# Reordering the first nine slots of a fused sparse-attention and feed-forward kernel

## Chip, cores and metric

The kernel runs on one core of a Trainium2 chip. The metric is the device time of one execution in microseconds (us). Its engines appear in the profile as PE (TensorE matmul), PEld (its weight loads), DVE (VectorE), ACT (ScalarE), POOL (GpSimd) and SP (SyncE, which here only issues DMAs). Each engine works through its own instructions strictly in the order in which the program gives them.

## What is computed

For 8 batches of 576 tokens with 8 heads of width 64, the reference computes causal attention. Heads 0 to 3 see the last 32 positions, heads 4 to 7 see the earlier positions of the same residue modulo 32. The result, 4608 tokens by 512, goes through a multiplicative feed-forward block:

```
scores = where(mask[h], q @ k.T / sqrt(64), -1e9)      # mask local for h < 4, strided for h >= 4
attn   = softmax(scores) @ v                            # (8, 8, 576, 64)
x      = attn.transpose(0, 2, 1, 3).reshape(4608, 512)
out    = ((x @ w1) * (x @ w2)) @ w3 @ w_out             # w1, w2: 512x1024; w3: 1024x1024; w_out: 1024x512
```

## The kernel before

**Slots.** The attention is cut into 32 pairs of heads (four pairs for each batch: two local, two strided). The main loop `for n in range(NP + 2)` has one slot for each pair, and a pair passes through the slots as a hand-written pipeline. For a pair, `load_qk` fetches q and k with a cast to fp16 (DMAs issued by POOL), `load_v` fetches v (issued by SP), and then:

- `emit_T` transposes q and k on PE (`tpq`, `tpk`) and copies them out as `qT`/`kT`. A local pair uses two ACT copies (L274). A strided pair uses one DVE copy `qTS` (L278) and one ACT copy (L279).
- `emit_S` makes the scores on PE (`sp`) and adds the mask on DVE in two halves (L305, `tmp`).
- `emit_max` and `emit_sub` are DVE passes (L313, L320), `emit_exp` is one ACT pass (L332).
- `emit_norm` takes row sums and reciprocals on DVE (L340, L342) and scales on POOL (L343).
- `emit_cast_v` casts v to fp16 on POOL (L254, `vh`).
- `emit_P` transposes the probabilities on PE (`pp`) and copies them on ACT (`pT`, L356 local, L363 strided).
- `emit_V` multiplies by v on PE (`op`) and copies into `xT`, on ACT for a local pair (L378), on ACT and DVE for a strided one (L392, L394, L396).

In a steady slot n of the kernel before, PE runs S(n), V(n-2), T(n+1), then P(n-1), with feed-forward pieces between them.

**Feed-forward pieces.** `w3 @ w_out` is folded once into one matrix `wfh`: for each of 8 row blocks `fold_t` transposes w3 on PE (`w3tp`, L207) and copies it on ACT (L209, `w3T`), and `fold_m` runs eight matmuls (`fps`, L216) and one ACT copy (L218, `wfh`). The tokens form 9 chunks of 512. For each chunk `emit_a` and `emit_b` run eight times each, four matmuls apiece (`aps` L225, `bps` L235). ACT copies a (L229, `asb`), DVE multiplies (L238, `abt`). `emit_out` runs four times per chunk, eight matmuls apiece (`ops`, L243), then an ACT copy (L246) and a store on SP.

**Credit.** `feed(us, batches)` hands out pieces in program order against a credit: `T_A` = 0.87 for an a or a b, twice that for an out or a `fold_m`, 0.6 for a `fold_t`. `next_piece` prefers a and b pieces whose tokens are complete (`full` counts finished batches), gives folds when there is none, and allows outs only when no fold is left. All of this happens when the program is built, so it sets each engine's order and nothing else.

**Shared buffers.** `psA` has two PSUM buffers, used by `tpq`, `tpk`, `pp` and `w3tp`; `psF` has six, used by all other matmuls. `s16`, the landing tile of q and k, has four. A DMA that POOL issues takes one of eight completion semaphores in turn, so that issue i waits on POOL until issue i-8 has landed.

## Time and profile before

| | |
|---|---|
| time, median of 3 runs | 309.9 us (309.56 to 310.26) |
| the profiled execution: its own time / its span | 311.65 us / 309.4 us |
| mean granted TensorE clock in it | 0.989 |
| busy: PE, DVE, ACT, POOL | 273.5, 187.1, 174.1, 145.3 us |
| chain that ended last: PE, DMA, DVE | 65%, 14%, 10% of the span |
| DMA: software queue (POOL), hardware queue (SP) | 14.88 MB, 21.24 MB |

The span is the time from the first to the last instruction of the profiled execution; the time of that execution has 2.25 us more around it. Busy time of PE counts overlapping matmuls once. Slots are told apart in the trace by their mask additions (`tmp`, L305) or their score matmuls (`sp`, L299).

### The profile page before, as it was taken

The page shows a single profiled execution, that of the slowest core. Times are in us where ns is not written, and L with a number is a line of the kernel's source. Part 1 is how long each engine was busy: PE and PEld are TensorE (multiplying, and loading weights), DVE is VectorE, ACT ScalarE, POOL GpSimd, SP SyncE. Part 2 cuts the span into 40 slices and gives each one's busy share as a digit, 9 for nine tenths or more (in the row PEclk, how much of TensorE's full clock was granted, in tenths as well). Part 3 has the DMA queues.
Part 4 walks back from the last instruction along what each step waited for, and adds up shares of the span by engine and source line. Part 5 has one row for each costly group of instructions (what it writes and reads, how often), then busy time and mean ns, then how long its engine had stood idle before and what let it go on. Part 6 is the DMA issues. An engine that isn't in the chain of part 4 may idle for free.

```text
span 309.4 us, 9098 instructions
## 1 busy us (share of the span) xinstructions
PE 273.5 (88%) x3793; PEld 148.4 (48%) x3793; DVE 187.1 (60%) x323; ACT 174.1 (56%) x303; POOL 145.3 (47%) x188
## 2 busy tenths in 40 slices
PE   1246668879999998999999999999999999999994
PEld 0235435545545554555555555545555544444442
DVE  2486333526988587668886876767787662342220
ACT  1535534768656655776676666756656654433332
POOL 8698634543665466456566436663764321000000
PEclk9999995999999999999999999999999999999999
DMA  8999999923446767656866667566844001100103
GB/s 147 201 183 207 205 204 183 168 49 70 78 79 129 155 128 133 133 119 122 183 127 124 117 131 166 115 136 143 159 78 124 36 0 70 68 2 34 68 34 136
DMA packets 64520, 36.69 MB, mean 119 GB/s; under 512 B 45792, under 2 KB 57824, under 8 KB 64480
## 3 DMA queue, kind: packets, MB, share of 16 engines
q0 software_dynamic: 26560, 14.88, 33.3%
q1 hardware_dynamic: 37920, 21.24, 25.2%
q8 instruction: 29, 0.48, 0.6%
q14 instruction: 11, 0.09, 0.1%
HBM read 41.43 MB, written 9.44 MB: 164 GB/s over the span
## 4 chain that ended last, share of the span: by engine, by line
PE 65%; DMA 14%; DVE 10%; ACT 3%; POOL 3%; issue 2%; SPq 1%; DVEq 0%; POOLq 0%; ACTq 0%
PE bps L235 17%; PE ops L243 17%; PE aps L225 16%; DMA s<-in_k_dram 9%; PE fps L216 4%; DVE tmp L305 3%; DMA s<-in_q_dram 3%; PE sp L299 3%; PE pp L355 2%; DMA vsS<-in_v_dram 2%; PE tpq L266 2%; PE op L375 2%; DVE abt L238 1%; DVE sm L340 1%; PE pp L360 1%
## 5 line engine op out<-in xcount | busy, mean ns | idle before, releaser
L238 DVE TENSOR_TENSOR abt<-bps,asb 128x512 f16<-128x512 f32 x72 | 49.5, 688 | 52.5 <-PE bps L235 32.5
L225 PE MATMUL aps<-xT,w1h 128*128 128x512 f16 x288 | 75.3, 380 | 0.9 <-DVE xT L396 0.4
L235 PE MATMUL bps<-xT,w2h 128*128 128x512 f16 x288 | 74.0, 379 | 0.0
L243 PE MATMUL ops<-wfh,abt 128*128 128x512 f16 x288 | 67.4, 379 | 1.3 <-DVE abt L238 1.3
L229 ACT COPY asb<-aps 128x512 f32<-128x512 f32 x72 | 42.1, 587 | 26.0 <-PE aps L225 25.9
L343 POOL TENSOR_TENSOR pr<-pr,rc 128x864 f16<-128x864 f16 x16 | 26.1, 1629 | 48.9 <-DVE rc L342 33.7
L243 PEld LDWEIGHTS <-abt 128*128 128x128 f16 x288 | 27.6, 98 | 35.2 <-DVE abt L238 3.7
L225 PEld LDWEIGHTS <-w1h 128*128 128x128 f16 x288 | 26.2, 98 | 31.1 <-DVE xT L396 4.1
L235 PEld LDWEIGHTS <-w2h 128*128 128x128 f16 x288 | 27.1, 98 | 29.3
L343 POOL TENSOR_TENSOR prS<-prS,rc 128x594 f16<-128x594 f16 x16 | 18.9, 1179 | 46.6 <-DVE rc L342 33.1
L246 ACT COPY osb<-ops 128x512 f32<-128x512 f32 x36 | 21.0, 587 | 27.2 <-PE ops L243 26.6
L320 DVE TENSOR_TENSOR tmp<-tmp,mx 128x864 f32<-128x864 f32 (+1 forms) x32 | 32.5, 1014 | 0.7
L305 DVE TENSOR_TENSOR tmp<-sp,maskL 128x480 f32<-128x480 f32 (+1 forms) x32 | 17.7, 595 | 21.7 <-PE sp L299 21.6
L332 ACT ACTIVATE pr<-tmp 128x864 f16<-128x864 f32 x16 | 14.8, 923 | 26.7 <-DVE tmp L320 26.7
L313 DVE TENSOR_REDUCE mx<-tmp 128x9 f32<-128x864 f32 (+1 forms) x32 | 29.0, 905 | 0.2
L266 PE MATMUL tpq<-id,s 54*64 54x54 f16 (+1 forms) x640 | 19.9, 200 | 9.3 <-DMA s<-in_q_dram 9.2
L340 DVE TENSOR_REDUCE sm<-pr 128x9 f32<-128x864 f16 x16 | 16.8, 1049 | 12.6 <-ACT pr L332 12.6
L266 PEld LDWEIGHTS <-s 54*64 54x64 f16 (+1 forms) x1280 | 16.6, 112 | 14.5 <-DMA s<-in_q_dram 9.6
L98 POOL DMA_DIRECT2D s<-in_k_dram x30 | 17.9, 604 | 11.3 <-DMA w1h<-in_moe_w_dram 3.5
L266 PE MATMUL tpk<-id,s 54*64 54x54 f16 (+1 forms) x640 | 19.6, 201 | 3.7 <-DMA s<-in_k_dram 3.7
L332 ACT ACTIVATE prS<-tmp 128x594 f16<-128x594 f32 x16 | 11.2, 702 | 17.6 <-DVE tmp L320 17.6
L98 POOL DMA_DIRECT2D s<-in_q_dram x30 | 19.1, 640 | 4.3 <-DMA w3s<-in_moe_w_dram 1.9
(65 smaller groups left out, 354.2 us busy)
## 6 DMA issues: line engine op xcount, KB each, us to landing
out_dram<-osb SPq DMA_DIRECT2D x36, 256.0 KB
vst<-in_v_dram SPq DMA_DIRECT2D x32, 192.0 KB
vsS<-in_v_dram SPq DMA_DIRECT2D x48, 54.0 KB
s<-in_q_dram POOLq DMA_DIRECT2D x16, 144.0 KB, 4.0
s<-in_k_dram POOLq DMA_DIRECT2D x16, 144.0 KB, 4.6
s<-in_q_dram POOLq DMA_DIRECT2D x30, 74.2 KB, 5.5
s<-in_k_dram POOLq DMA_DIRECT2D x30, 74.2 KB, 5.6
w3s<-in_moe_w_dram POOLq DMA_DIRECT2D x4, 512.0 KB, 13.1
```

Source lines behind the costliest of these rows:

```text
L98: nc.gpsimd.dma_start(t[p0:p0 + SW, h, :], _ap(src[b, h0 + h], 0, [[11 * D, 3], [NR * D, NA], [1, ST * D]]))
L225: nc.tensor.matmul(aps, w1h[:, ci, jc * P:(jc + 1) * P], xT[ci][:, c * NT:(c + 1) * NT], start=(ci == 0), stop=(ci == KC1 - 1))
L229: nc.scalar.copy(out=asb, in_=aps)
L235: nc.tensor.matmul(bps, w2h[:, ci, jc * P:(jc + 1) * P], xT[ci][:, c * NT:(c + 1) * NT], start=(ci == 0), stop=(ci == KC1 - 1))
L238: nc.vector.tensor_mul(abts[c][:, jc, :], bps, abts.pop((c, jc)))
L243: nc.tensor.matmul(ps, abts[c][:, jc, ts * P:(ts + 1) * P], wfh[:, jc, :], start=(jc == 0), stop=(jc == KC2 - 1))
L266: nc.tensor.transpose(tp[HALF * h:HALF * h + HALF, s, :], s16[p0:p0 + npar, h, s * D:(s + 1) * D], id16[p0:p0 + npar, p0:p0 + npar])
L305: nc.vector.tensor_tensor(out=tmp[:, t0:t1, :], in0=sp, in1=msk, op=ALU.add)
L313: nc.vector.tensor_reduce(out=mx, in_=tmp, axis=AX.X, op=ALU.max)
L320: nc.vector.tensor_tensor(out=tmp, in0=tmp, in1=_sub(mx, 0, P, 0, [[1, nt], [0, w]]), op=ALU.subtract)
L332: nc.scalar.activation(out=prv, in_=prs[i], func=AF.Exp, scale=SCALE)
L343: nc.gpsimd.tensor_tensor(out=prv, in0=prv, in1=_sub(rc, 0, P, 0, [[1, nt], [0, w]]), op=ALU.mult)
```

## The change

Only the order of the program changes, with the amounts handed to `feed`, and the engine of one copy. All of it lies in the preamble and in slots 0 to 8, except that the feed of later slots is 5.6 where it was 5.4.

- Preamble: `make_sel` goes ahead of `make_maskL`, and `load_qk(2)` behind both. `make_maskS` and the clearing of `prS` move from slot 0 into the preamble. `load_wo` and the first two `load_w3` leave it, `load_w12(0)` enters it.
- Loads: w1 and w2 are issued in the preamble and slot 0, wo in slot 2, w3 in slots 4 and 5. The loads of q, k and v for pairs 4 to 11 stand behind the `emit_norm` and `emit_cast_v` of a slot.
- Slots 1 to 4: `emit_V(n - 1)` directly behind `emit_P(n - 1)`, in place of `emit_V(n - 2)` behind `emit_S(n)`; slot 5 has none.
- Slots 3 to 7: `emit_T(n + 1)` at the very end of the slot, in place of behind `emit_S(n)`.
- Feed: nothing before slot 4. Chunk 0 is opened in slot 4, so that its sixteen a and b pieces come in slots 4 to 6, and the folds behind them in slots 6 to 8; the last of the folds stand behind chunk 1.
- The first pair's `qT` copy goes from ACT to DVE.

```diff
             for dst, tp in ((qT, tps[0]), (kT, tps[1])):
-                nc.scalar.copy(out=_sub(dst, 0, P, 0, [[LB, HALF], [1, LB]]),
-                               in_=_sub(tp, 0, P, 0, [[1, HALF], [HALF, LB]]))
+                eng = nc.vector.tensor_copy if i == 0 and dst is qT else nc.scalar.copy
+                eng(out=_sub(dst, 0, P, 0, [[LB, HALF], [1, LB]]),
+                    in_=_sub(tp, 0, P, 0, [[1, HALF], [HALF, LB]]))
...
         load_qk(1)
-        load_qk(2)
         for t in vsS:
             nc.vector.memset(t, 0.0)
         load_v(2)
         load_v(3)
+        make_sel()
         make_maskL()
-        make_sel()
+        load_qk(2)
+        for t in qTS + prS:
+            nc.vector.memset(t, 0.0)
+        make_maskS()
         emit_T(0)
-        load_wo()
         load_qk(3)
-        for t in qTS:
-            nc.vector.memset(t, 0.0)
         emit_cast_v(0)
-        load_w3(0)
-        load_w3(1)
+        load_w12(0)
         for n in range(NP + 2):
-            full = (n - 1) // 4 if n >= 6 else 0
-            f = (0.0, 0.0, 0.0, 4.6, 6.9, 5.9)[n] if n < 6 else 5.4
+            full = 0 if n < 5 else 1 if n == 5 else (n - 1) // 4
+            f = (0.0, 0.0, 0.0, 0.0, 3.0, 5.5, 5.5, 6.5, 6.5)[n] if n < 9 else 5.6
+            if n >= 9 and n + 3 < NP:
+                load_qk(n + 3)
+                load_v(n + 3)
             if n == 1:
                 load_qk(4)
-                load_v(4)
-                load_w3(2)
-                load_w3(3)
-            if n == 2:
-                load_w12(0)
-            if n == 3:
-                load_qk(5)
-                load_v(5)
-                load_w12(2)
-                load_qk(6)
-                load_v(6)
-            if n >= 4 and n + 3 < NP:
-                load_qk(n + 3)
-                load_v(n + 3)
+            if n == 8:
+                load_qk(10)
+                load_v(10)
             if n < NP:
                 emit_S(n)
-            if n > 1:
+            if n > 5:
                 emit_V(n - 2)
-            if n + 1 < NP:
+            if n + 1 < NP and (n < 3 or n > 7):
                 emit_T(n + 1)
...
             if 0 < n <= NP:
                 emit_P(n - 1)
+            if 0 < n < 5:
+                emit_V(n - 1)
+                full = n // 4
             feed(0.2 * f, full)
             if n < NP:
                 emit_norm(n)
                 if n + 1 < NP:
                     emit_cast_v(n + 1)
-            feed((0.4 if n > 3 else 0.8) * f, full)
+            if n == 0:
+                load_w12(2)
+            if n == 1:
+                load_qk(5)
+            if n == 2:
+                load_wo()
+                load_v(4)
+            if n == 3:
+                load_qk(6)
+                load_v(5)
+            if n == 4:
+                load_w3(0)
+                load_w3(1)
+                load_v(6)
+            if n == 5:
+                load_qk(7)
+                load_v(7)
+                load_w3(2)
+                load_w3(3)
+            if 5 < n < 9:
+                load_qk(n + 2 if n < 8 else 11)
+                load_v(n + 2 if n < 8 else 11)
+            feed((0.4 if n > 4 else 0.8) * f, full)
+            if 3 <= n <= 7:
+                emit_T(n + 1)
```

In the built program the order on PE from slot 4 on is: S4, P3, V3, four pieces, T5 | S5, two pieces, P4, four pieces, T6 | S6, V4, three pieces, P5, three pieces, one `fold_t`, T7 | S7, V5, then `fold_t` and `fold_m` three times each with P6 among them, T8 | S8, V6, T9, again three of each with P7 among them | S9.

More of the change, by code (lines that the diff above doesn't have):

```diff
@@ L452 @@
         load_v(3)
+        make_sel()
         make_maskL()
-        make_sel()
+        load_qk(2)
+        for t in qTS + prS:
+            nc.vector.memset(t, 0.0)
+        make_maskS()
         emit_T(0)
-        load_wo()
         load_qk(3)
-        for t in qTS:
-            nc.vector.memset(t, 0.0)
         emit_cast_v(0)
-        load_w3(0)
-        load_w3(1)
+        load_w12(0)
         for n in range(NP + 2):
-            full = (n - 1) // 4 if n >= 6 else 0
-            f = (0.0, 0.0, 0.0, 4.6, 6.9, 5.9)[n] if n < 6 else 5.4
+            full = 0 if n < 5 else 1 if n == 5 else (n - 1) // 4
[3 more added lines that the diff above has]
+                load_v(n + 3)
             if n == 1:
                 load_qk(4)
-                load_v(4)
-                load_w3(2)
-                load_w3(3)
-            if n == 2:
-                load_w12(0)
-            if n == 3:
-                load_qk(5)
-                load_v(5)
-                load_w12(2)
-                load_qk(6)
-                load_v(6)
-            if n >= 4 and n + 3 < NP:
-                load_qk(n + 3)
-                load_v(n + 3)
+            if n == 8:
+                load_qk(10)
+                load_v(10)
             if n < NP:
                 emit_S(n)
-            if n > 1:
+            if n > 5:
                 emit_V(n - 2)
-            if n + 1 < NP:
+            if n + 1 < NP and (n < 3 or n > 7):
                 emit_T(n + 1)
-            if n > 3:
+            if n > 4:
                 feed(0.1 * f, full)
@@ L491 @@
                 emit_max(n)
-            if n > 3:
+            if n > 4:
                 feed(0.15 * f, full)
@@ L496 @@
                 emit_exp(n)
-            if n == 0:
-                make_maskS()
-                for t in prS:
-                    nc.vector.memset(t, 0.0)
-            if n > 3:
+            if n > 4:
                 feed(0.15 * f, full)
```

## Prediction

> **What bounds the kernel now.** First the page's 40 slices (7.7 us each; PEclk is the granted clock in tenths):

> ```profile
> PE   1246668879999998999999999999999999999994
> PEclk9999995999999999999999999999999999999999
> DMA  8999999923446767656866667566844001100103
> ```

> From the tenth slice, 70 us, PE is full to the end; ahead of it PE has holes while the DMA engines are full. Busy time by stretches agrees (length, then PE, PEld, DVE, ACT, POOL, clock, DMA share, GB/s):

> ```profile
> 0.00:35.00 35.00, 12.37 (x335) 10.49 (x336) 19.25 (x33) 13.26 (x22) 29.19 (x49) 1.00 1.07 187
> 35.00:70.00 35.00, 28.31 (x392) 16.96 (x390) 13.86 (x21) 20.49 (x31) 14.70 (x19) 0.90 0.87 156
> 70.00:252.00 182.00, 179.86 (x2787) 96.83 (x2778) 138.18 (x243) 120.03 (x217) 99.79 (x120) 1.00 0.59 118
> ```

> So PE work done in the front needn't be done later, one for one. PE's timeline (start, length) shows the folds of the front, the first a piece, and where slot 9 begins:

> ```profile
> 37.43 3.34 PE L216 MATMUL fps<-woh,w3T 128*128 128x512 f16 x8
> 41.05 1.89 PE L216 MATMUL fps<-woh,w3T 128*128 128x512 f16 x8
> ...
> 70.00 1.04 PE L225 MATMUL aps<-xT,w1h 128*128 128x512 f16 x4
> ...
> 90.12 0.49 PE L299 MATMUL sp<-kT,qT 64*64 64x96 f16 x14
> ```

> The first eight fps took nearly twice as long as the next: the matmuls ran slow until about 40.4, some 5.1 us after PE's dense work began with the fold_t at 35.3.

> Last, DVE and ACT of slot 8. These durations are the unit prices below, and the brackets show that sm waits for exp (`pr`):

> ```profile
> 84.61 1.04 DVE L313 TENSOR_REDUCE mx<-tmp 128x9 f32<-128x864 f32 x1
> 85.69 1.06 DVE L320 TENSOR_TENSOR tmp<-tmp,mx 128x864 f32<-128x864 f32 x1
> 86.66 0.68 DVE L238 TENSOR_TENSOR abt<-bps,asb 128x512 f16<-128x512 f32 x1
> 87.79 1.05 DVE L340 TENSOR_REDUCE sm<-pr 128x9 f32<-128x864 f16 x1 [0.45 <-ACT pr L332]
> 86.84 0.92 ACT L332 ACTIVATE pr<-tmp 128x864 f16<-128x864 f32 x1 [1.46 <-DVE tmp L320]
> 88.35 0.59 ACT L229 COPY asb<-aps 128x512 f32<-128x512 f32 x1
> ```

> **The yardstick.** Where S9 begins, both programs have done S0 to S8, T0 to T9, P0 to P7, V0 to V6 and all of chunk 0. The kernel before has also done one more fold_t (0.61 us), two more fold_m (1.73 each) and an out (1.73): 5.8 us of PE. S9 starts at 90.1 before, so the change breaks even if S9 starts at 84.3. Behind S9 both orders have the same form and PE is the limit; feed 5.6 for 5.4 only takes pieces from the tail, where PE is full too. I walk the new order to S9.

> **Part 1: preamble, loads, S0.** k of pair 0 landed at 6.9. Putting four issues of qk2 (0.6 each) behind the masks ends maskL at 6.8, not 8.4; its two ACT copies (1.0) and kT (0.65) give S0 at 8.6 where it was 10.7. The DVE `qT` copy has no row: between `qTS` (0.46) and ACT's 0.65, beside those ACT copies, nothing. maskS's selects (0.5) and the memsets (prS 0.8) fit ahead of S0. qk2 issues 2.4 later but behind qk1 in a full queue (qk1 landed at 10.45), so still lands near 15.5. To qk4 the POOL queue carries the same weight bytes as before (w1 and w2 for wo and half of w3), so qk4 lands near 33 and w2's second half near 30. v4 and v5 are issued when their buffers come free, as before; at the traced rate (about 100 packets of 256 B each us beside weights, 1,728 a pair) v4 lands near 35, v5 near 45, each about when POOL reaches its cast. On SP the v loads keep their order among themselves and wait for those buffers wherever they stand; the first store comes long after v7, so moving them costs nothing. w3 is issued from 46 (behind cast 5), landing by 54, and by 71 for its second half: both ahead of their folds at 67 and 84. wo, issued near 29, has 40 us. No load holds PE up before T9.

> **Part 2: V(n-1) behind P(n-1), slots 1 to 4.** It makes a chain that the kernel before lacks. P's copy pT stands on ACT behind exp(n), V waits for pT, and S(n+1) stands on PE behind V:
> - Slot 0: S0 8.6 + mask wait 0.75, tmp 1.1, max 1.05, sub 1.06, exp 0.92, sm 1.05, rc 0.25: DVE reaches tmp1 at 14.8.
> - Slot 1: tmp1 to 15.9; T2 (qk2 at 15.5) and qTS to 17.0; max, sub, exp 3.05; first half of pT 0.65, V0 0.9: S2 at 21.6.
> - Slot 2: 0.5 + tmp 0.8, T3 and qTS 1.0, max 0.77, sub 0.8, exp 0.7, pT 0.7, V1 0.9: S3 at 27.8.
> - Slot 3: 0.5 + 0.8 + 0.77 + 0.8 + 0.7, pT 0.8, V2 0.5, T4 0.65, qT and kT 1.3: S4 at 34.7.
> - Slot 4: 0.45 + 1.12 + 1.05 + 1.06 + 0.92, pT 0.78, V3 0.5, xT casts 0.55: first a piece at 41.1.

> The subs of the front sometimes stretch beside POOL work (mean 1.23 against 1.06, once 3.1): 0.6 for all, so 41.7. The chunk starts 28 us earlier than before, but PE's first dense work 6 us later than the folds did.

> **Part 3: chunk 0 and T at the slot's end.** Four pieces are 3.45 warm. PE comes to them after 40 thin us; I take 5.1 us at half speed from the fps rows, +2.55 (bounds 0 and 3.45): 47.7. T5 0.65, qT and kT 1.25 with nothing for PE beside them: S5 at 49.6.

> Now T(n+1)'s copies close each slot's ACT and DVE order, and S(n+1) waits for all of it:
> - Slot 5: 0.45, tmp 1.1, max 1.05, abt 0.69, sub 1.06, exp 0.95, pT 1.15, asb 0.6, abt 0.7 (ahead of sm on DVE), sm 1.05, rc 0.25, abt 0.7, qTS 0.45 = 10.2 for 6.9 of PE work. S6 at 59.8.
> - Slot 6: to asb of the last a 7.0, w3T 1.0 behind it to 8.4 (T7 needs its psA buffer), T7 0.6, kT 0.7 = 9.8 for 8.0 of PE. S7 at 69.6.
> - Slot 7: S, V, P 1.4 and three folds 7.0; T8 beside the last wfh copy 0.6; behind that on ACT qT and kT 1.3 = 10.3 for 9.0 of PE. S8 at 79.9.
> - Slot 8: S, V, T9, P 1.8, folds 7.0, wait for qT of T9 0.75 = 9.5 without a DMA wait.
> - T9: qk9 is issued behind norm7 and cast 8: rc7 at 75.3, norm 1.2, cast 1.15, issue at 77.7 and 78.3; landing after 4.0 and 4.6 (medians of the page), 82.9. T9 is due at 80.8: +2.1 (bounds 0, if it lands in the fastest 3.2 and the slot is late, and 3.5). Behind the waiting T9 PE holds three folds, P7 and S9, and everything else waits for those.

> S9 at 91.5. Against 84.3 that is **7.2 us lost**, of which 3.3, 1.8, 1.3 and 2.7 are the waits of slots 5 to 8.

> [...]

> **The forecast.** 309.9 + 7.2 = 317.1, say 317.0, for the median. The profiled execution took 311.65 with a span of 309.4, 1.75 above the median; its own time should be near 319. Own range 313 to 320.5: 0.5 for each of slots 0 to 8, the cold start and T9 with their bounds.

> **Rivals.**
> - *The waits hide (faster).* If the copies behind T overlapped with PE work and PE were warm, slots 4 to 8 would take PE work alone: 41.1 + 4.1 + 6.9 + 8.0 + 9.0 + 8.9 = 78.0, 6.3 ahead of the yardstick, 303.6. It decides for faster once under half of the 13.5 us of waits remains (S9 ahead of 84.3). For: PE had under 1 us of idle a slot in slots 6 to 8 before. Against: T stood behind S there. Chance 0.15, most of it short of the full gain.
> - *The clock drops again (slower still).* The page shows 5 tenths in the seventh slice; the granted clock was 0.72 and 0.60 from 45 to 55, behind two waits of 2.2 and 0.8 at 43.6 to 46.9, which is half speed for (0.28 + 0.40) x 5 / 0.5 = 6.8 us. One such drop in slots 5 to 8 costs up to 3.4: 320.4; two, 323.8. Chance 0.25.
> - *It does nothing.* Feeding chunk 0 instead of folds only exchanges equal work, and the waits of the front merely change place: S9 within 0.6 of 84.3, 309.9. Chance 0.05.
> - My forecast: 0.55.

> Within 0.2% is 309.3 to 310.5, about what a measurement can tell from no change. Faster 0.15, same 0.05, slower 0.80. Leaving out the deeper half of the faster case and the end of the second drop, the range is 308.0 to 323.0.

> **What would show it.** Right: first aps at 40 to 44; S5, S6, S7, S8 starts 10 us apart; PE idle before S6 ended by DVE `qTS`, before S8 by ACT `kT`; T9 waiting for the DMA of k; S9 near 91. Wrong: S2 ahead of 20 or the first aps ahead of 38; slots 5 to 8 of 8 us; a stall on w1h, woh or w3s; or a steady part (S10 to S31) whose slots are not as long as before, 7 us, for then the yardstick fails.

## The result, and the profile after

The changed kernel takes **320.73 us** (median of 4 runs, 320.26 to 323.37), the kernel before beside it on the same chip 309.73 (309.55 to 310.26): a ratio of **1.037 [1.031, 1.043]**, 11.0 us slower. The profiled execution is the slowest of the four, 323.37 us with a span of 321.1 and a mean granted clock of 0.978 (0.983 in the other three), against 311.65, 309.4 and 0.989 before. The chips of the later runs gave the kernel before medians from 310.24 to 310.61, so experiments are compared by ratio, each against the kernel before on its own chip.

The page of the changed kernel, 40 slices of 8.0 us, tenths:

```profile
PE   0454388679499999999999989999999999999995
PEclk9999999798779999999999999999999999999999
DMA  8999989193817355956684666666764000100113
```

PE has its holes later than before (fourth and fifth slice, then the eighth, ninth and eleventh), and the clock drops in slices 8, 10, 11 and 12 (to 0.50 or 0.51 from 60.9 to 64.3, 71.2 to 74.6 and 84.8 to 91.6), where before it dropped once (0.50 from 47.2 to 54.0). The same stretches as before (length, PE, PEld, DVE, ACT, POOL, clock, DMA share, GB/s):

```profile
35.00:70.00 35.00, 25.34 (x318) 13.40 (x318) 18.11 (x29) 13.97 (x24) 16.87 (x20) 0.95 0.80 140
70.00:252.00 182.00, 174.66 (x2647) 96.05 (x2647) 123.63 (x216) 117.15 (x206) 96.30 (x119) 0.97 0.61 119
```

PE is busy for 3.0 us less from 35 to 70 than before (28.31) and for 5.2 less from 70 to 252 (179.86), and some of that is at half speed, in these three drops. PE's timeline after, with what ended each idle time in brackets:

```profile
41.16 0.52 PE L389 MATMUL op<-pT,vh 54*64 54x54 f16 x22 [4.02 <-ACT pT L364]
41.62 1.89 PE L225 MATMUL aps<-xT,w1h 128*128 128x512 f16 x4
...
49.71 0.57 PE L300 MATMUL sp<-kT,qT 64*64 64x96 f16 x18 [1.28 <-ACT kT L275]
...
59.48 0.53 PE L300 MATMUL sp<-kT,qTS 64*64 64x54 f16 x22 [2.91 <-DVE qTS L279]
...
69.44 0.21 PE L266 MATMUL tpk<-id,s 54*64 54x54 f16 x2 [0.96 <-ACT w3T L209]
...
70.75 0.53 PE L300 MATMUL sp<-kT,qTS 64*64 64x54 f16 x22 [0.79 <-ACT kT L280]
...
82.04 0.46 PE L300 MATMUL sp<-kT,qT 64*64 64x96 f16 x13 [1.35 <-ACT kT L275]
...
83.59 0.22 PE L266 MATMUL tpq<-id,s 64*64 64x64 f16 x2 [0.82 <-DMA s<-in_q_dram]
85.32 0.26 PE L266 MATMUL tpk<-id,s 64*64 64x64 f16 x2 [1.52 <-DMA s<-in_k_dram]
...
87.52 3.62 PE L216 MATMUL fps<-woh,w3T 128*128 128x512 f16 x8
...
94.23 1.89 PE L216 MATMUL fps<-woh,w3T 128*128 128x512 f16 x8
96.05 0.49 PE L300 MATMUL sp<-kT,qT 64*64 64x96 f16 x14
```

The `sp` lines are S5 to S9. S5 to S8 each begin behind a wait for a copy of their T; S9, whose T stands behind S8 again, does not, but T9 itself waited for its DMAs. The two `fps` lines are equal work, the first in the last clock drop (3.62 us at a clock of 0.50, against 1.89 at 1.00). S9 begins at 96.05, 11.75 behind the break-even point of 84.3. The two profiled executions differ by 323.37 - 311.65 = 11.72, so all that was lost was lost ahead of S9, as the yardstick has it.

Why S6 waits is seen on DVE and ACT in slot 5:

```profile
56.51 0.69 DVE L238 TENSOR_TENSOR abt<-bps,asb 128x512 f16<-128x512 f32 x1 [2.59 <-ACT asb L229]
57.12 1.04 DVE L341 TENSOR_REDUCE sm<-pr 128x9 f32<-128x864 f16 x1
...
58.97 0.45 DVE L279 COPY qTS<-tpq 128x594 f16<-128x594 f16 x1
54.01 0.92 ACT L333 ACTIVATE pr<-tmp 128x864 f16<-128x864 f32 x1 [2.14 <-DVE tmp L321]
54.84 1.15 ACT L357 COPY pT<-pp 96x640 f16<-96x640 f16 x2
55.89 1.07 ACT L229 COPY asb<-aps 128x512 f32<-128x512 f32 x2
```

T6's transposes were done on PE at 56.6. Their copy `qTS` is 0.45 us of work but the last of the slot on DVE: it comes only after exp, both halves of `pT`, `asb`, then `abt`, the row sums and one more `abt`.

### The profile page after: what moved, and what is told of

Read it like the earlier page. It is cut to its first block, busy times and chain, and to the rows that moved or that the text cites. A ratio compares the mean times of both kernels' runs of the same rounds, so it can differ in the third digit from the quotient of the medians.

```text
span 321.1 us, 9094 instructions
## 1 busy us (share of the span) xinstructions
PE 278.7 (87%) x3793; PEld 151.5 (47%) x3793; DVE 187.6 (58%) x324; ACT 173.2 (54%) x302; POOL 144.8 (45%) x188
## 4 chain that ended last, share of the span: by engine, by line
PE 69%; DMA 10%; DVE 9%; ACT 4%; issue 3%; POOL 2%; SPq 1%; ACTq 0%; POOLq 0%; DVEq 0%
PE aps L225 18%; PE bps L235 18%; PE ops L243 17%; DMA s<-in_k_dram 5%; PE fps L216 4%; PE sp L300 3%; DVE tmp L306 3%; DMA vst<-in_v_dram 2%; DMA vsS<-in_v_dram 2%; PE pp L356 2%; DVE abt L238 2%; PE op L376 2%; PE tpq L266 2%; DVE tmp L321 1%; PE pp L361 1%
## 5 line engine op out<-in xcount | busy, mean ns | idle before, releaser
L238 DVE TENSOR_TENSOR abt<-bps,asb 128x512 f16<-128x512 f32 x72 | 49.4, 688 | 62.8 <-PE bps L235 44.7
L225 PE MATMUL aps<-xT,w1h 128*128 128x512 f16 x288 | 77.6, 390 | 1.2 <-DVE xT L397 0.6
L235 PE MATMUL bps<-xT,w2h 128*128 128x512 f16 x288 | 76.0, 387 | 0.0
L229 ACT COPY asb<-aps 128x512 f32<-128x512 f32 x72 | 41.9, 588 | 27.2 <-PE aps L225 27.0
L235 PEld LDWEIGHTS <-w2h 128*128 128x128 f16 x288 | 28.1, 100 | 32.5 <-issue 2.4
L225 PEld LDWEIGHTS <-w1h 128*128 128x128 f16 x288 | 26.6, 100 | 31.4 <-DVE xT L397 3.4
L321 DVE TENSOR_TENSOR tmp<-tmp,mx 128x864 f32<-128x864 f32 (+1 forms) x32 | 30.2, 944 | 0.9
L333 ACT ACTIVATE pr<-tmp 128x864 f16<-128x864 f32 x16 | 14.8, 924 | 26.7 <-DVE tmp L321 26.7
L341 DVE TENSOR_REDUCE sm<-pr 128x9 f32<-128x864 f16 x16 | 16.8, 1050 | 10.8 <-ACT pr L333 10.8
L254 POOL CAST vh<-vst 96x1152 f16<-96x1152 f32 x16 | 18.8, 1173 | 0.0
```

Of the source, the lines that this page charges most:

```text
L225: nc.tensor.matmul(aps, w1h[:, ci, jc * P:(jc + 1) * P], xT[ci][:, c * NT:(c + 1) * NT], start=(ci == 0), stop=(ci == KC1 - 1))
L229: nc.scalar.copy(out=asb, in_=aps)
L235: nc.tensor.matmul(bps, w2h[:, ci, jc * P:(jc + 1) * P], xT[ci][:, c * NT:(c + 1) * NT], start=(ci == 0), stop=(ci == KC1 - 1))
L238: nc.vector.tensor_mul(abts[c][:, jc, :], bps, abts.pop((c, jc)))
L321: nc.vector.tensor_tensor(out=tmp, in0=tmp, in1=_sub(mx, 0, P, 0, [[1, nt], [0, w]]), op=ALU.subtract)
L333: nc.scalar.activation(out=prv, in_=prs[i], func=AF.Exp, scale=SCALE)
```

## Experiments

Times of the experiments are medians, and a point is 1% of the time of the kernel before. Two causes are to be told apart from one another and from the clock. **Theory:** T(n+1) at the slot's end exposes its copies on DVE and ACT, and qk9, issued late, stalls T9; nearly all the loss is there. **Rivals:** the chunk-first order itself, or V(n-1) in place of V(n-2), sets the loss, and T's place only shows it.

### T back behind S, and the loads a slot earlier

```diff
-            if n + 1 < NP and (n < 3 or n > 7):
+            if n + 1 < NP and n != 3:
                 emit_T(n + 1)
...
-            if 3 <= n <= 7:
+            if n == 3:
                 emit_T(n + 1)
# q and k of pair 7 issued in slot 4 (was 5), 8 in 5, 9 in 6, 10 in 7; 11 stays in 8
```

> The changed kernel, but T(n+1) stands behind S(n) again in slots 4 to 8 (only T4 stays at its slot's end), and so that its data is there, q and k of pairs 7 to 11 are loaded one slot earlier. Theory (the waits behind T at the slots' ends cost the time, 3.3 + 1.8 + 1.3 us in slots 5 to 7, 1.3 ahead of S5, and the T9 wait of 2.3; the half clock in slots 6 to 8 comes from those waits and goes with them): 8 to 10 us of the 11 come back, 310 to 313 us, S9 near 86, no clock drop between 50 and 92. Rival 1 (the front is late because V(n-1) stands behind P(n-1) and nothing else matters): within 2 us of 320.7. Rival 2 (the order of the loads costs it): no gain, and w3, now behind more loads, costs 1 to 2 us more.

309.67 us, ratio **1.0003 [0.9967, 1.0039]**: all 11 us are back, with chunk 0 still first and V(n-1) still in slots 1 to 4. In the profile S5 to S9 begin at 47.0, 53.8, 62.5, 72.1 and 81.3, the clock is 1.0, and from 41 to 96 the longest waits of PE are these (us in total, times, longest):

```profile
PE op L389 <- ACT pT L364: 2.8, 1, 2.8
PE w3tp L207 <- ACT qT L275: 1.5, 2, 0.7
PE tpk L266 <- DMA s<-in_k_dram: 0.9, 3, 0.4
```

The waits of S on `qTS` and `kT` are gone. Six of the ten executions had next to no half speed (clock 0.998 to 1.0, 308.5 to 310.0 us) and four had some (0.993 to 0.994, 311.2 to 312.0); every execution of the kernel before beside them had some (0.987 to 0.993). So the two kernels are level in the median, but not with equal clocks. The theory holds for T and the loads together; the next runs part them.

### The loads alone

```diff
# as above for q and k of pairs 7 to 10; T(n+1) stays at the slot's end
```

> The changed kernel with the loads of e1 alone (q and k of pairs 7 to 11 a slot earlier); T stays at the slots' ends. It parts e1's two edits. Theory (T's place is worth some 8 of the 11 us, the loads only T9's wait): as e2, 317 to 319. Rival (e1 gained by its loads): 309.5 to 313.

316.16 us, ratio **1.0206 [1.0159, 1.0253]**. S9 begins at 87.0. T9 no longer waits for its load, the waits behind T are the old ones:

```profile
PE sp L300 <- DVE qTS L279: 2.9, 1, 2.9
PE sp L300 <- ACT kT L275: 2.6, 2, 1.4
PE tpk L266 <- ACT w3T L209: 1.0, 1, 1.0
```

So, taken away in this order, the 3.70 points of the change divide into 1.64 points (5.1 us) for the late loads and 2.03 points (6.3 us) for T's place; T early beside the late loads was not run. Of the first, T9's wait itself was 2.3 us. The rest fits the clock: this profile has one half-speed stretch, 57.4 to 60.8, where the changed kernel had three, and three of the four executions had a clock of 0.995, by 2 x (1 - clock) x span an estimated 3.1 us at half speed, where three of the four of the changed kernel had 0.983, an estimated 10.8. Slots 7 and 8, S7 to S9, had no drop and no wait for a load here, and took 9.75 and 9.0 us:

```profile
68.27 0.53 PE L300 MATMUL sp<-kT,qTS 64*64 64x54 f16 x22 [0.79 <-ACT kT L280]
...
78.02 0.46 PE L300 MATMUL sp<-kT,qT 64*64 64x96 f16 x13 [1.35 <-ACT kT L275]
...
87.02 0.48 PE L300 MATMUL sp<-kT,qT 64*64 64x96 f16 x14
```

### Only qk9 earlier

```diff
             if 5 < n < 9:
-                load_qk(n + 2 if n < 8 else 11)
+                if n == 6:
+                    load_qk(8)
+                    load_qk(9)
+                if n == 8:
+                    load_qk(11)
```

> The changed kernel, but q and k of pair 9 are issued with those of pair 8 in slot 6, so that T9 finds its data. Theory: the 2.3 us that PE waits around T9 go, and the half clock from 84.8 to 91.6 with them (up to 3.4 us more): 315 to 318.5 us. If the clock drops anyway, because the wait ahead of S8 is enough for it: 318.4. Rival (the wait only moves to the qT copy of T9 or to the folds behind): 320.7 within 0.7.

318.12 us, ratio **1.0258 [1.0228, 1.0289]**, 1.1 points (3.5 us) better than the changed kernel. In the profile T9 waits for nothing, S9 begins at 88.7, and only one drop is left, 59.5 to 62.9; slots 7 and 8 are again free of drops, at 9.7 and 9.0 us. But the profiled execution is the fastest of the four (316.68 us, clock 0.995); the others had clocks of 0.982 to 0.989, two of them as much half speed as the changed kernel. By the intervals, it is not shown that taking 2.3 us of waiting away brought more than 2.3 us.

### V two slots back

```diff
-            if n > 5:
+            if n > 1:
                 emit_V(n - 2)
...
-            if 0 < n < 5:
-                emit_V(n - 1)
-                full = n // 4
# feed 0 in slot 4, 6.75 in slots 5 to 8; T stays at the slot's end
```

> The changed kernel, but V(n-2) stands behind S(n) in slots 2 to 5 as in the kernel before, so that S(n+1) no longer stands behind V(n-1), and chunk 0 opens in slot 5; the feed of slots 5 to 8 is 6.75 each (27 in all as in the changed kernel), T stays at the slots' ends. Theory (the chain S, exp, pT, V, S sets slots 1 to 4): S4 is still bound by q and k of pair 4, which landed at 33.5, so S4 near 35; S5 near 41 to 43, first a piece near 42 to 44, with S5 already issued: 2 to 6 us better than the changed kernel, 315 to 319. Rival (the front is bound by loads and by DVE, not by V's place): S5 and the first a piece later than 46, and the time 320.7 or more.

316.54 us, ratio **1.0185 [1.0155, 1.0216]**. S2 and S3 come 3 to 4 us earlier (18.9 and 24.9), but what they gained runs into q of pair 4 and into the probabilities' copy:

```profile
32.34 0.26 PE L266 MATMUL tpq<-id,s 64*64 64x64 f16 x2 [3.11 <-DMA s<-in_q_dram]
...
41.04 0.26 PE L266 MATMUL tpk<-id,s 64*64 64x64 f16 x2 [3.84 <-ACT pT L364]
```

The first a piece comes at 44.1, later than with V(n-1). It gains 1.85 points all the same; S6 now waits 1.1 us for `qTS`, not 2.9. The feed had to move with V, so it is V(n-1) together with its feed that is not free beside a late T; which of the two it is, no run here tells. With T early:

### T early, loads earlier and V two back together

```diff
# the edits of the first and of the last experiment in one kernel
```

> The changed kernel with both e1's edit (T behind S in slots 4 to 8, q and k of pairs 7 to 11 a slot earlier) and e3's (V two slots back, feed 6.75 in slots 5 to 8): what is left of the change is the order of the weights, chunk 0 ahead of the folds, and the preamble. Theory (the two prices add: 11 and 4 to 5 back): S5 near 41 to 43, S9 near 76 to 80, 304 to 307 us, faster than both kernels. Rival (with PE no longer waiting, v's loads, POOL's casts or DVE set slots 4 to 8): S9 at 81 or later, 309 or more.

312.55 us, ratio **1.0066 [1.0045, 1.0087]**: 0.63 points (2 us) *slower* than with V(n-1). The prices do not add, as the rival said. Here T6 comes so early that it waits for a load issued behind wo, ahead of every piece of chunk 0:

```profile
43.75 0.25 PE L266 MATMUL tpq<-id,s 54*64 54x54 f16 x1 [2.42 <-DMA s<-in_q_dram]
44.77 0.25 PE L266 MATMUL tpq<-id,s 54*64 54x54 f16 x1 [0.76 <-DMA s<-in_q_dram]
```

So V two slots back, with its feed, gained beside a late T and lost beside an early one, where PE waits for a load instead.

### The late T in the kernel before

```diff
-            if n + 1 < NP:
+            if n + 1 < NP and not 4 <= n <= 7:
                 emit_T(n + 1)
...
             feed((0.4 if n > 3 else 0.8) * f, full)
+            if 4 <= n <= 7:
+                emit_T(n + 1)
```

> The kernel before with one part of the change alone: T(n+1) at the end of slots 4 to 7. Loads, feeds and V as before. Theory (T at the end makes S(n+1) wait for copies behind all of the slot's ACT and DVE work): 1 to 3 us of PE wait ahead of each of S5 to S8, and possibly a clock drop of 3.4: 314 to 320 us. Rival (T's place is free, since PE has pieces enough, and the change lost its time in the front and by its loads): within 1 us of 309.7.

310.12 us, ratio **1.0005 [0.9972, 1.0039]**. By itself this speaks for the rival, for T late seems to cost nothing. The waits of PE from 41 to 96 tell why not:

```profile
PE sp L299 <- ACT kT L274: 2.7, 2, 1.4
...
PE sp L299 <- ACT kT L279: 1.6, 2, 0.8
```

The waits behind T are there, 4.3 us of them. But T5, which in the kernel before waited 2.2 and 0.8 us for its q and k at 43.6 to 46.9, comes after its data here, and the clock drop that followed (0.50 from 47.2 to 54.0) is not in the profile; 7 of 10 executions had none. Those 7, at a clock of 1.0, took 309.2 to 311.0 us, the other 3 (0.989 to 0.994) 312.3 to 312.6. The edit had taken a loss away as well as added one, so it was cut down to the slots in which T waits for no load:

```diff
# as before, but with 5 <= n <= 7
```

> The kernel before with T(n+1) at the end of slots 5 to 7 only, so that T5 keeps its wait for q and k of pair 5 (3.7 us in the kernel before, which e4 was rid of, along with the clock drop behind it). Theory (T at a slot's end costs S(n+1) the wait for its copies, which e4 showed as 0.8, 0.8 and 1.35, and e4 came out level only because T5 no longer waited): 311.5 to 314, with the drop near 47 in place. Rival (the wait behind T is free because the work ahead of it comes sooner): 309.5 to 311.

312.42 us, ratio **1.0059 [1.0033, 1.0085]**, 1.8 us slower. The waits behind T are 0.8, 0.8 and 1.35, T5's load wait (2.1 and 0.9 us) and a drop behind it (47.6 to 51.0) are back. So a late T costs in the old order too, and the clocks (0.989 to 0.994, beside 0.987 to 0.992 of the kernel before) show no more half speed for it: beside 2.95 us of waits it took 1.8 longer. It costs less than in the changed kernel, where DVE and ACT end slots 5 and 6 with chunk 0's `abt` and `asb` work and T6 alone exposes 2.9; that this is the reason is argued, not shown.

### Slot 4 alone

```diff
# T(n+1) at the slot's end for n == 4 only, in the kernel before
```

> The kernel before with T(n+1) at the slot's end in slot 4 alone, so that the folds of slot 4 come ahead of T5's wait for its loads. It is the part by which e4 differs from e8. Theory (a T at the end costs its copies' wait, 1.35 us here, but spares a wait for loads where there is one, 3.7 us around T5, and the clock drop behind it, 3 us): if the parts add, e4 less e8, about 1.8 us better than before in the median, 308 to 309. Rival (e4 and e8 differ by the chance of the clock's windows): level with before within 0.6.

309.52 us, ratio 0.9976 [0.9951, 1.0000]. T5's wait went, and in its place PE waited 2.1 us for POOL's scaling ahead of P3 and 1.35 for `kT` ahead of S5. The clock drop moved from 47.2 to 55.8 instead of going. The parts of the two runs above do not add: their difference promised 1.8 us, and 0.7 came, with an interval that reaches 1.

### Filler matmuls

What share is the clock's? Dummy matmuls (128x512, into an unused `psF` buffer) keep PE busy while it waits. First in the changed kernel, 8 ahead of V3, 5, 12, 3 and 5 behind T5 to T8, 3 ahead of T9:

```diff
+    def warm(k):
+        ps = psF.tile([P, NT], FP32, tag="f", name="warm")
+        for j in range(k):
+            nc.tensor.matmul(ps, w1h[:, 0, 0:P], w1h[:, 0, 0:NT], start=True, stop=True)
```

> The changed kernel with extra matmuls (128x512, on w1, their result is never read) where PE waits: 8 ahead of V3, 5, 12, 3 and 5 behind T5, T6, T7 and T8, 3 ahead of T9; nothing else is changed. They are 36 x 0.216 = 7.8 us of work when warm, inside waits of 4.0, 1.3, 2.9, 0.8, 1.4 and 0.8 us. Theory (the half clock in slots 6 to 8 follows from PE's idle time and cost 3 to 5 us of the 11): no drop between 50 and 92, four pieces of chunk 0 not at 0.42 us a matmul throughout, 314.5 to 318.5 us although work is added. Rival (the clock is not set by these waits, or its drops fall beside other waits): 320.7 to 323.

318.57 us, ratio **1.0269 [1.0228, 1.0311]**, 1.0 point (3.1 us) better. The dummies take the slow start on themselves:

```profile
36.54 3.29 PE L446 MATMUL warm<-w1h 128*128 128x512 f16 x8
40.77 0.37 PE L389 MATMUL op<-pT,vh 54*64 54x54 f16 x22 [0.94 <-ACT pT L364]
41.08 1.05 PE L225 MATMUL aps<-xT,w1h 128*128 128x512 f16 x4
```

Eight dummies at 0.41 us each, then a first piece of 1.05 where the changed kernel's took 1.89; S5 comes at 46.4 for 49.7. Two drops of 3.4 us remain, at 66.7 and 83.7, behind waits for loads, of T7 (1.5 us, which the changed kernel did not have) and of T9 (1.9).

Then in the kernel of the first experiment (T early), 3 dummies ahead of P3 and 7 ahead of V3:

> e1 with extra matmuls (128x512 on w1, never read) in slot 4 alone: 3 ahead of P3 and 7 ahead of V3, in waits of 0.7 and 2.8 us that PE has there. Theory (the four pieces of slot 4 ran at half speed in the changed kernel and in e1, 0.42 us a matmul, about 3.4 us in all, and e5 brought S5 forward by 3.3 with such matmuls): the pieces of slot 4 warm, S5 near 44, S9 near 78 to 79, 306 to 308 us, faster than both kernels. Rival (S5 to S9 in e1 are set by DVE, ACT and loads, so that an earlier start is eaten up by S9): 309 to 310.

308.92 us, ratio 0.9962 [0.9934, 0.9990]. S5 is 3.3 us earlier, S9 only 0.6: T7 now came ahead of its loads, and a drop (0.50 from 54.4 to 57.8) followed it.

```profile
53.23 0.21 PE L266 MATMUL tpk<-id,s 54*64 54x54 f16 x1 [0.72 <-DMA s<-in_k_dram]
53.87 0.21 PE L266 MATMUL tpk<-id,s 54*64 54x54 f16 x1 [0.43 <-DMA s<-in_k_dram]
...
54.33 1.86 PE L225 MATMUL aps<-xT,w1h 128*128 128x512 f16 x4
```

Then in the kernel before: 4 dummies ahead of T4, 8 ahead of T5 (which waits for its load there) and 3 behind it:

> The kernel before with extra matmuls (128x512 on constants, never read): 4 ahead of T4, 8 ahead of T5 and 3 behind it, where PE waited 1.7, 2.2 and 0.7 us for loads and copies. Theory (the drop from 47.2 to 54.0 in the kernel before follows from the wait for q and k of pair 5, and costs its 3.4 us): no drop, 306 to 307.5 us, as much better as the undropped executions of e4 were than its dropped ones (3 us). Rival (the clock looks at more than these waits): level with 309.7 within 1 us, drop still there.

**308.51 us, ratio 0.9942 [0.9913, 0.9970]**, the lowest median of all and below both kernels (the run ahead of it, 308.92, is within its interval). Six of its eight executions had a clock of 0.997 or more (307.5 to 308.7 us); the other two, the profiled one among them, 0.992 to 0.993 (309.5 and 310.7). In the profile, T5's wait is covered in part and the drop behind it lasts 3.4 us (47.0 to 50.4), where it lasted 6.8:

```profile
41.16 1.90 PE L445 MATMUL warm<-wz,id 128*128 128x512 f16 x8
44.54 0.22 PE L266 MATMUL tpq<-id,s 64*64 64x64 f16 x2 [1.47 <-DMA s<-in_q_dram]
```

Last, 4 dummies ahead of T4 in the kernel of "slot 4 alone":

> e11 with 4 extra matmuls ahead of T4 (on constants, never read), so that the folds of slot 3 begin warmer. Theory: as e11 and another 0.5 to 2 us, 306.5 to 308, the fastest of all. Rival (the matmuls push T4 back, whose copies P2 and the folds wait for): as e11 or up to 1 us slower.

309.44 us, ratio 0.9973 [0.9949, 0.9996], as without them. The drop stayed (54.5 to 61.3), and so did the waits for `prS` and `kT`.

## Why the prediction was right, and where its sum fell short

The kernel is slower, by the mechanism named, and the time lies in the range. The likeliest figure, 317.0, is 3.7 us low, and the forecast's own range ended 0.2 below the measured 320.7.

- **The yardstick** held: 11.75 us at S9, 11.72 on the whole. The slots behind S9 needed no account.
- **Slots 0 to 4** were right almost to the tenth in the sum: first a piece at 41.62 (predicted 41.7), S5 at 49.71 (49.6). Single steps were off by up to a microsecond and made up for each other, which is luck: S0 at 9.2 (8.6), S2 at 22.55 (21.6), S3 at 28.1 (27.8), S4 at 35.5 (34.7). Four pieces took 6.4 for 6.0, a matmul every 0.42 us.
- **The loads**: w2's second half landed at 31.7 (30), qk4 at 33.5 (33). From slot 4 on, no load but that of pair 9 held PE up (in slot 3, T4 waited 0.33 us for its k).
- **Slot 5**: 9.77 us for 10.2, closed by `qTS` as said, through the chain that was written out.
- **T9**: 0.82 + 1.52 = 2.3 us of wait for 2.1. Its q was issued at 80.23 and landed after 3.3, its k at 80.87 and landed after 4.4. The rows of before, 4.0 and 4.6, were 0.7 too long for q, but within 0.2 for the k that T9 waited for last. Issue and T9 were each 2 to 3 us later than predicted, so that the wait between them came out the same is luck too.
- **Slots 6, 7 and 8** are where the sum failed: 11.3, 11.3 and 14.0 us for 9.8, 10.3 and 11.6 (the last with T9's wait). The errors are +1.5, +1.0 and +2.4, 4.9 in all (the terms of slot 6 as written add up to 9.3, or 9.7 from the 8.4, not 9.8). The mis-sized term is the clock: the likeliest case had no drop behind the cold start, two drops of 6.8 us were the second rival's limit (323.8), and the profile has three, 60.9 to 64.3, 71.2 to 74.6 and 84.8 to 91.6. Together they are 13.6 us at half speed (clock 0.50 to 0.51), as much as the rival's two, an estimated 6.8 us of PE work lost at most, where the kernel before lost up to 3.4 in its one. Against the 9.7 and 9.0 us that slots 7 and 8 take without drops, the changed kernel's 11.3 leaves 1.6 for the drop in slot 7, and its 14.0 leaves 2.7 beside T9's wait of 2.3; the forecast was 0.5 to 0.6 too high for both slots without drops. The rival's mechanism came true on top of the forecast's, not in place of it. Its chance of 0.25 looks too low: waits of 3.3, 1.8, 1.3 and 2.7 us in slots 5 to 8 stood in the forecast itself, and each of the three drops begins inside a wait of those slots or within 1.5 us behind it. In the other three executions an estimated 10.8 us at half speed, up to 5.4 of work, would cover the 3.7 us by which the median was missed.
- **"The waits hide"** was wrong by the brackets of S5 to S8, and the run with T early shows the price: 2.03 points.
- **"It does nothing"**, for equal work is exchanged, was right on the net of what is left: with T and the loads early the changed kernel equals the one before within [0.9967, 1.0039], though with less half speed. What chunk 0's order, V(n-1) and the preamble each cost was not told apart there, and they may cancel.

What stays open: how much of the 6.3 us of T's place is wait and how much clock. From the first a piece to S9, the profiles with the loads alone and with T early show (as above, length, then PE first):

```profile
40.49:87.02 46.53, 38.45 (x538) 21.55 (x534) 23.42 (x40) 27.14 (x44) 21.90 (x26) 0.96 0.71 130
41.98:81.26 39.28, 36.61 (x502) 20.48 (x498) 22.76 (x40) 26.17 (x42) 22.01 (x26) 1.00 0.84 147
```

PE is idle for 8.1 us in the first and 2.7 in the second, so in these two the waits are 5.4 us, and the first one's drop of 3.4 us (57.4 to 60.8) is, as an estimate, up to 1.7 us of PE work. But drops fall differently in each execution (those of the kernel before with T late lie 2.9 us apart with and without one, medians 312.5 and 309.6), and no run of the changed order has the waits without a drop, so the shares in the median are not shown.

## To carry to other kernels

In a hand-ordered pipeline, put a step's transposes where the engines that copy them out have least queued ahead, not where PE has its last gap: 0.45 us of copy cost 2.9 us because it stood last in DVE's order. Count a wait of PE once for its length, and look whether the clock drops behind it as it did here (to 0.50 for 3.4 or 6.8 us, by estimate up to 1.7 or 3.4 us of PE work, though not behind every wait); and ask of each load that is issued later whether the slot that uses it comes later too. The prices of the moves did not add here (V two slots back gained 1.85 points beside a late T and lost 0.63 beside an early one): take each away alone and together, and look which wait is last next.

## What the hardware showed

```profile
57.45:60.86 3.41, 1.38 (x43) 1.06 (x44) 2.80 (x7) 0.59 (x3) 2.22 (x2) 1.00 0.00 0
60.86:64.27 3.41, 3.41 (x10) 1.24 (x9) 1.44 (x3) 0.76 (x2) 3.41 (x7) 0.51 0.39 56
67.80:71.20 3.40, 1.66 (x75) 1.51 (x73) 1.37 (x4) 1.67 (x2) 3.08 (x4) 1.00 1.14 210
81.40:84.80 3.40, 0.94 (x42) 0.82 (x42) 2.32 (x5) 1.08 (x3) 2.51 (x5) 1.00 1.10 193
```

The drops start at 60.9, 71.2 and 84.8, which are 3 and 4 times 3.4 us apart, and last 3.4, 3.4 and 6.8 us. PE was busy for 40%, 49% and 28% of the stretches ahead of them. In eleven profiles the clock dropped (before, after and nine experiments), to 0.50 for 3.4 or 6.8 us each time. Cut into stretches of 3.41 us from each one's first drop on, and back to 43 us, these profiles show: of the stretches at full clock, all ten with PE busy for less than 45% were followed by half speed, none above 63% was, and of those between some were and some not (49%, 52%, 55% and 62% were; 48%, 52%, 54%, 57% and others were not). That is a count over these profiles; what sets the clock they do not show. As an estimate from these rows, 3.4 us at a clock of 0.51 cost up to 1.7 us of PE work. Executions of one kernel, the one before with T late, stood 2.9 us apart with and without half speed (medians 312.5 and 309.6).

PE's first pieces ran slow as well. The changed kernel's first piece began at 41.62, with its matmuls 0.42 us apart, and from about 47.3 on, 5.7 us later, they stood 0.22 apart; with the loads earlier the first piece began at 40.5 and the 0.22 came from 43.8 on, after 3.3 us. In both profiles that is 13.6 us, four times 3.4, ahead of the first drop (60.9 and 57.4). The recorded clock says 1.00 through both: the slow start is seen only in the matmuls.
